# The opening of a fused attention and token-mixing kernel: eight score pairs in one written order for all engines

## The chip, the cores and the metric

The kernel runs on one core of one Trainium2 chip. A core has TensorE (PE; its weight loads are listed as PEld), VectorE (DVE), ScalarE (ACT), GpSimd (POOL) and SyncE (SP, which here only issues DMAs). The metric is the device time of one execution in microseconds (us), lower is better, as the median of several runs. Times inside a run count from the start of its span, which goes from the first to the last instruction.

## What is computed

Two blocks follow each other, for 8 batches of 3200 tokens, 256 columns wide:

```python
# u, v: (8, 3200, 256), z: (8, 3200, 64), float32
scores = (1 / 3200) * z @ z.transpose(0, 2, 1)
attn = np.maximum(scores, 0.0) ** 2
x = u * (attn @ v)                       # gated attention
wq, wk = x @ w_q, x @ w_k                # w_q, w_k: (256, 64)
W_tok = 0.125 * einsum('bsd,btd->bst', wq, wk)
mixed = einsum('bst,btd->bsd', W_tok, x)
out = np.maximum(mixed, 0.0) @ w_out     # w_out: (256, 256)
```

## The kernel before

**Tiles.** The 3200 tokens of a batch are 25 tiles of 128 rows. Columns of the score matrix are taken in groups of 512 (six, and one of 128). For one group, a score tile is 128 x 512: z of one row tile against z of the group's columns, over 64 entries. Two score tiles make a pair, which fills one PSUM buffer of 128 x 1024 float32; there are three such buffers (tag `ps`). Scores use z transposed, kept twice in `zT` (in partitions 0 to 63 and 64 to 127), so that the two tiles of a pair use the two halves of TensorE's rows.

**One pair** n passes four steps, which this text names by a letter and the pair's number:

- s (`scores`, L275): 64-row matmuls into a `ps` buffer.
- e (`first_stage`): relu and scaling into `g`, float32, on ScalarE (L287) or VectorE (L289). It frees the `ps` buffer.
- q (`second_stage`): the square, float16 into `at`, on ScalarE (L298) or GpSimd (L300). Where the score tile's transpose serves a later group, a DMA on SP's queue (L317) transposes it right behind.
- m (`second_product`, L333): `at` times v, accumulated over all tiles of the group in two PSUM banks, `acc0` and `acc1`. A tile makes four products of 128 x 256.

After a group's last product the gate (L463 to L466) multiplies by u, and the token-mixing work of the second block is worked in later.

**Order.** The schedule is written by hand: every engine takes its instructions in the order in which the program emits them, and semaphores are added for the data and the buffers. A loop over phases k emits, in each, some score pairs, their e, the q of the pairs of the phase before, and products of earlier pairs. From phase 3 on, products run as 64-row matmuls in two lanes, with score pairs between them. Loads and casts of later data are put on a list by phase (`due`). Products of the first group come in portions of 2, 4, 4, 5, 5 and 5 tiles (`first_sizes`), from phase 1 on.

**The opening.** z of the first batch comes in four chunks of 4, 6, 7 and 8 tiles (`ZCH`), which cover tiles 0 to 3, 12 to 17, 18 to 24 and 4 to 11; the first group takes its tiles in this order. Per chunk c there are three steps: z (`cast_first`, L113: two casts to float16, one for each copy), t (`turn_first`, L122: one TensorE transpose per tile) and c (the copy into `zT`, L126). Chunks 0 and 1 are turned in `acc0` and `acc1`, chunks 2 and 3 in `ps` buffers. So s0 and s1 need c0, s2 to s4 need c1, s5 to s7 need c2. v of the first batch is loaded in four DMAs with a cast, issued by GpSimd (L101).

The program emits: the identity, the four z loads (on SP), v tiles 0 to 3, then z0, t0, c0, z1, z2, v 12 to 17, z3, v 18 to 24, v 4 to 11. Phase 0 emits s0 s1, e0 e1, t1 c1, q0 q1. Phase 1: s2 s3 s4, e2 e3 e4, t2 c2, q2 q3 q4, m0. Phase 2: s5 s6 s7, e5 e6 e7, t3 c3, m1 m2. Phase 3 begins with the first u load on SP's queue, s8 (pair 8), e8, q5 q7 (GpSimd) and q6 (ScalarE), then products of pairs 3 and 4 with s9 and s10 between them. ScalarE has e0 c1 q0 e2 q2 q4 e5; VectorE has c0 e1 e3 e4 c2 e6 e7 c3; GpSimd has q1 and q3, and all casts of z2 and z3. The casts of z0 are on VectorE and ScalarE, those of z1 on ScalarE and GpSimd.

`zeros` is a 128 x 256 tile used later as a filler operand; GpSimd clears it in phase 11 (L206).

Of the kernel before, what the change touches and what calls it, by code (L numbers as in the profile page):

```python
# [9 lines left out]
FP16 = mybir.dt.float16  # L10
# [6 lines left out]
def kernel(  # L17
# [10 lines left out]
    nc = tc.nc  # L28

    B, S, D = u.shape  # L30
    dqk = z.shape[2]
    dh = moe_w_q.shape[1]
    P = 128
    NT = S // P
    ND = D // P
    W = 512
# [5 lines left out]
    LAG = 2  # L42
# [20 lines left out]
    pat = ctx.enter_context(tc.tile_pool(name="pat", bufs=NAT))  # L63
# [4 lines left out]
    pps = ctx.enter_context(tc.tile_pool(name="pps", bufs=3, space=bass.MemoryType.PSUM))  # L68
# [5 lines left out]
    def acc_tile(half, name, dtype=FP32):  # L74
        n = W if dtype == FP32 else 2 * W
        return pacc.tile([P, n], dtype, tag=f"acc{half}", name=name)

    ctx.enter_context(tc.manual_schedule())

    zT, vs, us, xs, xTs, qks, ks, hacc, hss, rts, zds = ({} for _ in range(11))  # L80
# [5 lines left out]
    ZCH = [(0, 4), (12, 6), (18, 7), (4, 8)]  # L86
# [8 lines left out]
    def load_first_z():  # L95
        for n0, nn in ZCH:
            z32[n0] = px.tile([P, nn, dqk], FP32, tag="x_sb", name="z32")
            nc.sync.dma_start(out=z32[n0][:], in_=rows(z, 0)[:, n0 : n0 + nn, :])

    def load_first_v(n0, nn):  # L100
        nc.gpsimd.dma_start(out=vs[0][:, n0 : n0 + nn, :], in_=rows(v, 0)[:, n0 : n0 + nn, :])  # L101

    def cast_first(c):
        n0, nn = ZCH[c]
        casts = [
            (nc.vector.tensor_copy, nc.scalar.copy),
            (nc.scalar.copy, nc.gpsimd.tensor_copy),
            (nc.gpsimd.tensor_copy, nc.gpsimd.tensor_copy),
            (nc.gpsimd.tensor_copy, nc.gpsimd.tensor_copy),
        ][c]  # L110
        zd0[c] = pat.tile([P, nn, 2, dqk], FP16, tag="at", name="zd")
        for half, cast in enumerate(casts):
            cast(out=zd0[c][:, :, half, :], in_=z32[n0][:])  # L113

    def turn_first(c):
        n0, nn = ZCH[c]
        if c < 2:
            tp = acc_tile(c, "ztp", FP16)
        else:
            tp = pps.tile([P, 4 * W], FP16, tag="ps", name="ztp")  # L120
        for i in range(nn):
            nc.tensor.transpose(  # L122
                tp[:, ts(i, P)], zd0[c][:, i, :, :].rearrange("p a k -> p (a k)"), ident
            )
        copy = nc.scalar.copy if c == 1 else nc.vector.tensor_copy
        copy(out=zT[0][:, ds(n0 * P, nn * P)], in_=tp[:, 0 : nn * P])  # L126

# [48 lines left out]
    def load_u(b, gi):  # L178
        n0, nn = starts[gi] // P, widths[gi] // P
        us[b, gi] = pu.tile([P, 4, D], FP32, tag="u_sb", name="u_sb")  # L180
        nc.sync.dma_start(out=us[b, gi][:, 0:nn, :], in_=rows(u, b)[:, n0 : n0 + nn, :])
# [22 lines left out]
    def clear(*tiles_):  # L204
        for tile_ in tiles_:
            nc.gpsimd.memset(tile_, 0.0)  # L206
# [57 lines left out]
    def scores(p0):  # L264
        pair = tiles[p0 : p0 + 2]
        sc = ps_tile("sc")
        ats = [[], []]
        for h, (b, gi, tis) in enumerate(pair):
            w = widths[gi]
            half = h * dqk  # L270
            for i in range(W // w):
                ti = tis[min(i, len(tis) - 1)]
                ats[h].append((i * w, h, w, b, ti, starts[gi], half))
        for at, h, w, b, ti, gs, half in sorted(ats[0] + ats[1]):
            nc.tensor.matmul(  # L275
                out=sc[:, h, at : at + w],
                lhsT=zT[b][half : half + dqk, ds(z_at(b, h) + ti * P, P)],
                rhs=zT[b][half : half + dqk, ds(z_at(b, h) + gs, w)],
                start=True,
                stop=True,  # L280
            )
        return sc

    def first_stage(p0, sc, on_act):
        g = pg.tile([P, 2, W], FP32, tag="g", name="g")
        if on_act:
            nc.scalar.activation(out=g[:], in_=sc[:], func=RELU, scale=GSCALE)  # L287
        else:
            nc.vector.tensor_scalar(  # L289
                out=g[:], in0=sc[:], scalar1=0.0, scalar2=GSCALE, op0=AOP.max, op1=AOP.mult  # L290
            )
        return g

    def second_stage(p0, g, on_act):
        at = pat.tile([P, 2 * W], FP16, tag="at", name="at")
        out = at[:].rearrange("p (a w) -> p a w", a=2)
        if on_act:
            nc.scalar.square(out=out, in_=g[:])  # L298
        else:
            nc.gpsimd.tensor_mul(out=out, in0=g[:], in1=g[:])  # L300
        blocks = []
        for h, (b, gi, tis) in enumerate(tiles[p0 : p0 + 2]):
            for i, ti in enumerate(tis):
                made[b, gi, ti] = (at, h * W + i * widths[gi])
            gj = group_of(tis[0])
            if is_turned(gi, gj):
                blocks.append((b, gi, gj, tis[0] - starts[gj] // P, 1, h * W, (h + 1) * W))
        if len(blocks) == 2 and blocks[0][:3] == blocks[1][:3] and blocks[1][3] == blocks[0][3] + 1:
            blocks = [blocks[0][:4] + (2, blocks[0][5], blocks[1][6])]
        for b, gi, gj, n0, nn, c0, c1 in blocks:  # L310
            if (b, gi, gj) not in turned:
                bufs = {1: 3, 2: 4, 4: 1}[gj - gi]
                turned[b, gi, gj] = ptt.tile(
                    [P, 4, 4, P], FP16, tag=f"tt{gj - gi}", name=f"tt{gj - gi}", bufs=bufs
                )
            out = turned[b, gi, gj][:].rearrange("p n j t -> p (n j) t")
            nc.sync.dma_start_transpose(out=out[:, 4 * n0 : 4 * (n0 + nn), :], in_=at[:, c0:c1])  # L317
# [19 lines left out]
    def whole(banks):  # L337
        return [
            lambda i=i: i.emit(ALL, i.start, i.stop) for bank in banks for i in bank
        ]  # L340
# [80 lines left out]
    def second_product(b, gi, rows_, first, last):  # L421

        nj = widths[gi] // P
        split = is_split(b, gi)
        if first:
            for half in range(2 if split else (nj + 1) // 2):
                accs[half] = acc_tile(half, f"acc{half}")

        def item(ti, j, half):
            return Item(  # L430
                out=accs[half][:, ds((j % 2) * D, D)],
                lhsT=lambda r: weights(b, gi, ti, j, r),
                rhs=lambda r: vs[b][r, ti, :],
                start=(first and ti == rows_[0] and j % 2 == 0),
                stop=(last and ti == rows_[-1] and (j % 2 == 1 or j == nj - 1)),
            )

        if split:
            return [[item(ti, 0, half) for ti in rows_] for half in range(2)]
        return [  # L440
            [item(ti, j, half) for ti in rows_ for j in range(2 * half, min(2 * half + 2, nj))]
            for half in range(2)
        ]
# [268 lines left out]
    def due(k, fn):  # L712
        at_phase.setdefault(k, []).append(fn)
# [84 lines left out]
    now = [0]  # L798
    mixed_at = [-9]
    make_identity(nc, ident)  # L800
    load_first_z()
    load_first_v(0, 4)
    cast_first(0)
    turn_first(0)
    cast_first(1)
    cast_first(2)
    load_first_v(12, 6)
    cast_first(3)
    load_first_v(18, 7)
    load_first_v(4, 8)  # L810
    due(3, lambda: load_u(0, 0))
    due(6, load_weights)
    due(8, load_out_weights)
    due(10, cast_weights)
    due(11, lambda: clear(zeros[:], zr[:, NT, :], first_kx[0][:]))
    due(12, lambda: double_weights(0))
    due(14, lambda: double_weights(1))
    due(15, lambda: clear(*[t[:] for t in first_kx[1:]], *[t[0:dh, :] for t in hz]))
# [54 lines left out]
        key += "x" if mixing else "k" if keying else "p" if projecting else ""  # L873
        return shares_of[key][:n]

    made_by = []
    waiting = []
    produced = consumed = k = 0
    groups = [(b, gi) for b in range(B) for gi in range(NG)]
    left, steps, across = None, 0, False  # L880
    gate_pending = False
    while groups:
        now[0] = k
        for fn in at_phase.pop(k, []):
            fn()
        n = 4 if k == 0 else 6
        mixing = None
        if len(groups) <= 2 and NTILE - produced <= 4 and not key_due(k):
            while todo_mix:
# [34 lines left out]

        for p0, sc in fresh:
            stage(p0, sc)
        if k < 3:
            turn_first(k + 1)
        if k < 2:

            for i, (p0, g) in enumerate(staged):
                second_stage(p0, g, i != 1)
            staged = []
        if len(waiting) == 3:
            second_on_act = [False, True, k % 2 == 0]
        else:
# [10 lines left out]
        while asides:  # L947
            asides.pop(0)()

        if k == 0:  # L950
            k += 1
            continue
        ready = made_by[k - (1 if k < 3 else LAG)]
        b, gi = groups[0]
        if begins:
            group_begun(k, b, gi)
            need = ends[b, gi]
            scored = tiles[consumed:need]
            scored = [t for _, _, tis in scored for t in tis]
            left = [t for t in range(NT) if t not in scored]  # L960
            first_sizes = [2, 4, 4, 5, 5, 5] if k == 1 else []
        need = ends[b, gi]
        rest = len(left) + sum(len(tis) for _, _, tis in tiles[consumed:need])
        if first_sizes:
# [180 lines left out]
```

## Time and profile before

| | us |
|---|---|
| median of 3 runs (lowest to highest) | 796.01 (794.72 to 796.9) |
| profiled execution, time | 793.18 |
| profiled execution, span | 790.8 |
| TensorE busy in the span | 769.5 |
| first TensorE instruction (t0) | 3.39 |
| first TensorE instruction of phase 3 (s8) | 15.39 |
| first gate, TensorE's last product before it ends near | 26.3 |

In the profile a busy engine is one with an instruction in flight; matmuls are pipelined, so a group's duration holds the wait of its last result too. "idle before" is what the engine waited just ahead of a group, with what released it. The granted clock (PEclk) is that of TensorE, as a share of full speed. A row of a timeline joins neighbouring instructions of one kind: start, duration of the whole, engine, line, operation, written and read tiles, shapes, count. In a row of stretches each engine has its busy time and its count of instructions, in the order TensorE, weight loads, VectorE, ScalarE, GpSimd, then the granted clock, the DMA engines' share and GB/s.

### The profile page before, as it was taken

To read this page: it belongs to the slowest core of one execution; us is meant where nothing else is said; L and a number is where in the kernel's file an instruction comes from. 1 tells how busy PE (TensorE), PEld (TensorE's weight loads), DVE (VectorE), ACT (ScalarE), POOL (GpSimd) and SP (SyncE) were. 2 spreads that over 40 slices of the span, in tenths; PEclk is the share of its full clock that TensorE was granted. 3 is DMA by queue.
4 is the path that set the end of the run, shared out by engine and by line. 5 is a ranking of instruction groups with operands and counts; after the bars stand their busy time and mean duration, and the time that the engine had idled before them with its cause. 6 is when DMAs were issued, how large, how long until landed. Compare 5 with 4: busy or idle time off the path is not lost. (4 is left out here: it accounts for less than half of the span.)

```text
span 790.8 us, 28408 instructions
## 1 busy us (share of the span) xinstructions
PE 769.5 (97%) x12590; PEld 658.3 (83%) x12590; DVE 470.4 (59%) x455; ACT 559.8 (71%) x656; POOL 552.6 (70%) x364
## 2 busy tenths in 40 slices
PE   7999999999999999999999999999999999999996
PEld 4777878887888888889878997899988998887884
DVE  5655566646655567555756457655575646665444
ACT  6766677776778776685867657758687877675465
POOL 7888698667766587774869658885677536876350
PEclk9999999999999999999999999999999999999999
DMA  8999799984999869995799949899489994988526
GB/s 170 179 210 206 124 201 194 190 185 82 237 184 216 173 157 216 231 229 138 171 214 235 241 114 177 222 188 262 113 216 187 228 229 97 189 193 165 157 61 257
DMA packets 276266, 147.03 MB, mean 186 GB/s; under 512 B 252080, under 2 KB 255664, under 8 KB 276144
## 3 DMA queue, kind: packets, MB, share of 16 engines
q1 hardware_dynamic: 275424, 143.33, 84.8%
q0 software_dynamic: 576, 1.64, 1.3%
q8 instruction: 98, 1.61, 0.9%
q10 hardware_dynamic: 144, 0.26, 0.1%
q14 instruction: 24, 0.20, 0.1%
HBM read 59.38 MB, written 26.21 MB: 108 GB/s over the span
## 5 line engine op out<-in xcount | busy, mean ns | idle before, releaser
L289 DVE TENSOR_SCALAR g<-sc 128x1024 f32<-128x1024 f32 x338 | 411.3, 1222 | 265.0 <-PE sc L275 235.8
L333 PE MATMUL acc<-v_sb,at 64*128 64x256 f16 (+1 forms) x7387 | 482.8, 269 | 3.6 <-POOL at L300 1.4
L300 POOL TENSOR_TENSOR at<-g 128x1024 f16<-128x1024 f32 x239 | 446.7, 1893 | 12.8 <-DVE g L289 12.0
L333 PEld LDWEIGHTS <-at 64*128 64x128 f16 (+1 forms) x7387 | 388.7, 94 | 68.4 <-PE acc L333 18.4
L298 ACT ACTIVATE at<-g 128x1024 f16<-128x1024 f32 x229 | 236.7, 1054 | 17.2 <-DVE g L289 16.2
L466 POOL TENSOR_TENSOR x_sb<-gt,u_sb 128x512 f16<-128x512 f32 x48 | 61.2, 1275 | 195.0 <-ACT gt L463 180.8
L333 PE MATMUL acc<-v_sb,tt 64*128 64x256 f16 (+1 forms) x2540 | 179.0, 269 | 0.0
L275 PE MATMUL sc<-zT 64*128 64x512 f16 (+1 forms) x1104 | 168.2, 346 | 3.2 <-ACT g L287 1.6
L287 ACT ACTIVATE g<-sc 128x1024 f32<-128x1024 f32 x130 | 133.0, 1023 | 41.0 <-PE sc L275 35.4
L333 PEld LDWEIGHTS <-tt 64*128 64x128 f16 (+1 forms) x2540 | 135.4, 94 | 10.1
L275 PEld LDWEIGHTS <-zT 64*128 64x128 f16 x1104 | 60.0, 94 | 11.1 <-issue 3.5
L600 ACT ACTIVATE rt<-mx 128x1024 f16<-128x1024 f32 x47 | 47.8, 1023 | 27.3 <-PE mx L579 25.3
L463 ACT COPY gt<-acc 128x512 f32<-128x512 f32 x48 | 28.1, 586 | 46.8 <-PE acc L333 46.7
L333 PE MATMUL fo<-wo,rt 64*128 64x256 f16 (+1 forms) x688 | 59.4, 269 | 1.3 <-DVE g L289 0.7
L661 ACT ACTIVATE fo<-fo 128x1024 f32<-128x1024 f32 (+2 forms) x44 | 43.6, 999 | 20.0 <-PE fo L333 19.6
L501 ACT CAST qk<-qk 128x512 f16<-128x512 f32 x47 | 27.5, 585 | 40.7 <-PE qk L333 40.4
L333 PE MATMUL qk<-x_sb,kx 64*128 64x256 f16 x368 | 55.0, 269 | 0.8 <-DVE g L289 0.8
L333 PEld LDWEIGHTS <-rt 64*128 64x128 f16 (+1 forms) x688 | 41.1, 94 | 13.4 <-issue 3.2
L464 DVE TENSOR_TENSOR x_sb<-acc,u_sb 128x512 f16<-128x512 f32 x48 | 33.1, 690 | 27.4 <-PE acc L333 24.5
L333 PEld LDWEIGHTS <-kx 64*128 64x128 f16 (+1 forms) x386 | 36.2, 94 | 7.1 <-DMA kx<-ql 0.7
L333 PE MATMUL qk<-xT_sb,wkq 64*128 64x512 f16 (+1 forms) x90 | 31.7, 376 | 0.8 <-DMA xT_sb<-x_sb 0.8
L333 PE MATMUL qk<-xT_sb,wqk 64*128 64x512 f16 (+1 forms) x94 | 30.1, 376 | 0.0
(79 smaller groups left out, 260.3 us busy)
## 6 DMA issues: line engine op xcount, KB each, us to landing
u_sb<-in_u_dram SPq DMA_DIRECT2D x48, 512.0 KB, 5.1
out_dram<-fo SPq DMA_DIRECT2D x45, 512.0 KB, 3.6
piece<-in_v_dram SPq DMA_DIRECT2D x42, 512.0 KB, 4.6
piece<-in_z_dram SPq DMA_DIRECT2D x7, 512.0 KB, 5.6
tt<-at SPq DMA_TRANSPOSE x162, 4.9
piece<-in_z_dram SPq DMA_DIRECT2D x7, 288.0 KB, 5.7
out_dram<-fo SPq DMA_DIRECT2D x5, 256.0 KB, 2.7
u_sb<-in_u_dram SPq DMA_DIRECT2D x8, 128.0 KB, 3.3
```

What stands on the lines that cost most here:

```text
L275: nc.tensor.matmul(out=sc[:, h, at : at + w], lhsT=zT[b][half : half + dqk, ds(z_at(b, h) + ti * P, P)], rhs=zT[b][half : half + dqk, ds(z ...
L287: nc.scalar.activation(out=g[:], in_=sc[:], func=RELU, scale=GSCALE)
L289: nc.vector.tensor_scalar(out=g[:], in0=sc[:], scalar1=0.0, scalar2=GSCALE, op0=AOP.max, op1=AOP.mult)
L298: nc.scalar.square(out=out, in_=g[:])
L300: nc.gpsimd.tensor_mul(out=out, in0=g[:], in1=g[:])
L333: return nc.tensor.matmul(out=self.out, lhsT=self.lhsT(rows), rhs=self.rhs(rows), start=start, stop=stop)
L463: nc.scalar.copy(out=upper[:], in_=accs[1][:])
L464: nc.vector.tensor_mul(out=x[:, 0:n], in0=accs[0][:, 0:n], in1=ug[:, 0:n])
L466: nc.gpsimd.tensor_mul(out=x[:, n : 2 * n], in0=upper[:], in1=ug[:, n : 2 * n])
L501: nc.scalar.copy(out=qks[b, gi][:, 0:gw], in_=out)
L600: nc.scalar.activation(out=out, in_=ps[:], func=RELU)
L661: nc.scalar.mul(out=flat_out[:, sl], in_=part, mul=FINAL_SCALE)
```

## The change

The opening, up to s7, is no longer emitted by phases 0 to 2 but by a new function `opening`, which reads one string of words. A word is a step (z, t, c, v, s, e, q, m), a number, and the engine (A ScalarE, D VectorE, P GpSimd); for z the digit between them is the copy, and "w10" is ten products of zeros on TensorE into `acc1` (128 x 256 each). `turn_first` is parted into the transposes and `place_first`, the copy. The loop then starts at phase 3 with the counters that phases 0 to 2 left.

What differs in order: ten products of zeros ahead of t0 and three behind it; t1 and c1 ahead of s0; t2 and m0 ahead of s4, t3 and m1 ahead of s5, m2 ahead of s7 (per engine; the words of different engines only stand side by side). The v loads of tiles 12 to 17 and 18 to 24 stand ahead of z2's casts on GpSimd, the last v load behind z3's casts. c1 goes from ScalarE to VectorE, q1 from GpSimd to ScalarE, e3 from VectorE to ScalarE. `zeros` is cleared on VectorE at the start instead of on GpSimd in phase 11.

```diff
--- before.py
+++ after.py
@@ -75,6 +75,11 @@
         n = W if dtype == FP32 else 2 * W
         return pacc.tile([P, n], dtype, tag=f"acc{half}", name=name)
 
+    OPENING = """
+        v0 z00D z01A w10 t0 w2 w1 c0D z10A z11P t1 c1D v1 s0 s1 e0A v2 e1D z20P z21P q0A s2
+        e2D q1A z30P z31P s3 e3A t2 m0 s4 c2D q2A v3 e4D q3P t3 m1 c3D s5 e5A q4A s6 e6D m2
+        s7 e7D
+    """
     ctx.enter_context(tc.manual_schedule())
 
     zT, vs, us, xs, xTs, qks, ks, hacc, hss, rts, zds = ({} for _ in range(11))
@@ -100,30 +105,29 @@
     def load_first_v(n0, nn):
         nc.gpsimd.dma_start(out=vs[0][:, n0 : n0 + nn, :], in_=rows(v, 0)[:, n0 : n0 + nn, :])
 
-    def cast_first(c):
+    cast_by = {"A": nc.scalar.copy, "D": nc.vector.tensor_copy, "P": nc.gpsimd.tensor_copy}
+    ztp = {}
+
+    def cast_first(c, half, by):
         n0, nn = ZCH[c]
-        casts = [
-            (nc.vector.tensor_copy, nc.scalar.copy),
-            (nc.scalar.copy, nc.gpsimd.tensor_copy),
-            (nc.gpsimd.tensor_copy, nc.gpsimd.tensor_copy),
-            (nc.gpsimd.tensor_copy, nc.gpsimd.tensor_copy),
-        ][c]
-        zd0[c] = pat.tile([P, nn, 2, dqk], FP16, tag="at", name="zd")
-        for half, cast in enumerate(casts):
-            cast(out=zd0[c][:, :, half, :], in_=z32[n0][:])
+        if half == 0:
+            zd0[c] = pat.tile([P, nn, 2, dqk], FP16, tag="at", name="zd")
+        cast_by[by](out=zd0[c][:, :, half, :], in_=z32[n0][:])
 
     def turn_first(c):
         n0, nn = ZCH[c]
         if c < 2:
-            tp = acc_tile(c, "ztp", FP16)
-        else:
-            tp = pps.tile([P, 4 * W], FP16, tag="ps", name="ztp")
+            ztp[c] = acc_tile(c, "ztp", FP16)
+        else:
+            ztp[c] = pps.tile([P, 4 * W], FP16, tag="ps", name="ztp")
         for i in range(nn):
             nc.tensor.transpose(
-                tp[:, ts(i, P)], zd0[c][:, i, :, :].rearrange("p a k -> p (a k)"), ident
-            )
-        copy = nc.scalar.copy if c == 1 else nc.vector.tensor_copy
-        copy(out=zT[0][:, ds(n0 * P, nn * P)], in_=tp[:, 0 : nn * P])
+                ztp[c][:, ts(i, P)], zd0[c][:, i, :, :].rearrange("p a k -> p (a k)"), ident
+            )
+
+    def place_first(c, by):
+        n0, nn = ZCH[c]
+        cast_by[by](out=zT[0][:, ds(n0 * P, nn * P)], in_=ztp[c][:, 0 : nn * P])
 
 
 
@@ -798,21 +802,11 @@
     now = [0]
     mixed_at = [-9]
     make_identity(nc, ident)
-    load_first_z()
-    load_first_v(0, 4)
-    cast_first(0)
-    turn_first(0)
-    cast_first(1)
-    cast_first(2)
-    load_first_v(12, 6)
-    cast_first(3)
-    load_first_v(18, 7)
-    load_first_v(4, 8)
     due(3, lambda: load_u(0, 0))
     due(6, load_weights)
     due(8, load_out_weights)
     due(10, cast_weights)
-    due(11, lambda: clear(zeros[:], zr[:, NT, :], first_kx[0][:]))
+    due(11, lambda: clear(zr[:, NT, :], first_kx[0][:]))
     due(12, lambda: double_weights(0))
     due(14, lambda: double_weights(1))
     due(15, lambda: clear(*[t[:] for t in first_kx[1:]], *[t[0:dh, :] for t in hz]))
@@ -873,17 +867,62 @@
         key += "x" if mixing else "k" if keying else "p" if projecting else ""
         return shares_of[key][:n]
 
-    made_by = []
-    waiting = []
-    produced = consumed = k = 0
+
+
     groups = [(b, gi) for b in range(B) for gi in range(NG)]
-    left, steps, across = None, 0, False
+    begun = {}
+
+    def warm(n):
+        if "x" not in begun:
+            begun["x"] = acc_tile(1, "sc")
+        for _ in range(n):
+            nc.tensor.matmul(
+                out=begun["x"][:, 0:D], lhsT=zeros[:, 0:P], rhs=zeros[:], start=True, stop=True
+            )
+
+    def opening(order):
+        sc, g = {}, {}
+        for word in order.split():
+            what, n, by = word[0], int(word[1:2]), word[2:]
+            if what == "z":
+                cast_first(n, int(by[0]), by[1])
+            elif what == "t":
+                turn_first(n)
+            elif what == "c":
+                place_first(n, by)
+            elif what == "v":
+                load_first_v(*[(0, 4), (12, 6), (18, 7), (4, 8)][n])
+            elif what == "s":
+                sc[n] = scores(2 * n)
+            elif what == "e":
+                g[n] = first_stage(2 * n, sc.pop(n), by == "A")
+            elif what == "q":
+                second_stage(2 * n, g.pop(n), by == "A")
+            elif what == "w":
+                warm(int(word[1:]))
+            elif what == "u":
+                load_u(0, 0)
+            elif what == "m":
+                ti = [t for x in tiles[2 * n : 2 * n + 2] for t in x[2]]
+                for fn in whole(second_product(0, 0, ti, n == 0, False)):
+                    fn()
+        return [(2 * n, g[n]) for n in sorted(g)]
+
+    load_first_z()
+    nc.vector.memset(zeros[:], 0.0)
+    waiting = opening(OPENING)
+    made_by = [4, 10, 16]
+    produced, consumed, k = 16, 6, 3
+    group_begun(1, 0, 0)
+    steps = 6
+    across = False
+    left, first_sizes = [], [4, 5, 5, 5]
     gate_pending = False
     while groups:
         now[0] = k
         for fn in at_phase.pop(k, []):
             fn()
-        n = 4 if k == 0 else 6
+        n = 6
         mixing = None
         if len(groups) <= 2 and NTILE - produced <= 4 and not key_due(k):
             while todo_mix:
@@ -924,13 +963,6 @@
 
         for p0, sc in fresh:
             stage(p0, sc)
-        if k < 3:
-            turn_first(k + 1)
-        if k < 2:
-
-            for i, (p0, g) in enumerate(staged):
-                second_stage(p0, g, i != 1)
-            staged = []
         if len(waiting) == 3:
             second_on_act = [False, True, k % 2 == 0]
         else:
@@ -947,10 +979,7 @@
         while asides:
             asides.pop(0)()
 
-        if k == 0:
-            k += 1
-            continue
-        ready = made_by[k - (1 if k < 3 else LAG)]
+        ready = made_by[k - LAG]
         b, gi = groups[0]
         if begins:
             group_begun(k, b, gi)
@@ -958,7 +987,6 @@
             scored = tiles[consumed:need]
             scored = [t for _, _, tis in scored for t in tis]
             left = [t for t in range(NT) if t not in scored]
-            first_sizes = [2, 4, 4, 5, 5, 5] if k == 1 else []
         need = ends[b, gi]
         rest = len(left) + sum(len(tis) for _, _, tis in tiles[consumed:need])
         if first_sizes:
```

## The prediction

> **What bounds the kernel now.** I read the page's busy table first, then stretches of the opening, then each engine's timeline up to 20 us. Times within the run count from the start of its span.
>
> ```profile
> PE 769.5 (97%) x12590; PEld 658.3 (83%) x12590; DVE 470.4 (59%) x455; ACT 559.8 (71%) x656; POOL 552.6 (70%) x364
> ```
>
> TensorE is the bound. Its idle 21 us (790.8 - 769.5) include 5.9 of the first 15.39 us (15.39 - 9.50 busy). The second row below is the stretch behind: 11.00 of 11.00 us busy.
>
> ```profile
> 0.00:15.39 15.39, 9.50 (x65) 5.36 (x66) 7.78 (x9) 9.03 (x10) 11.64 (x19) 1.00 0.79 153
> 15.39:26.39 11.00, 11.00 (x178) 8.26 (x179) 9.23 (x8) 9.36 (x10) 8.97 (x5) 1.00 1.08 168
> ```
>
> So a change of the opening is worth what it moves TensorE's first instruction of phase 3, score pair s8, now at 15.39, if the helpers then keep up. TensorE's timeline (start, duration, operation):
>
> ```profile
> 3.39 0.61 PE L122 MATMUL ztp<-ident,zd 128*128 128x128 f16 x4 [3.39 <-ACT zd L113]
> 4.51 1.04 PE L275 MATMUL sc<-zT 64*128 64x512 f16 x4 [0.52 <-DVE zT L126]
> 5.48 0.82 PE L122 MATMUL ztp<-ident,zd 128*128 128x128 f16 x6
> 7.19 1.46 PE L275 MATMUL sc<-zT 64*128 64x512 f16 x6 [0.89 <-ACT zT L126]
> 9.06 0.91 PE L122 MATMUL ztp<-ident,zd 128*128 128x128 f16 x7 [0.41 <-ACT g L287]
> 9.76 1.91 PE L333 MATMUL acc<-v_sb,at 128*128 128x256 f16 x8
> 11.60 0.82 PE L275 MATMUL sc<-zT 64*128 64x512 f16 x6
> 13.11 0.61 PE L122 MATMUL ztp<-ident,zd 128*128 128x128 f16 x8 [0.69 <-ACT g L287]
> 13.55 1.91 PE L333 MATMUL acc<-v_sb,at 128*128 128x256 f16 x16
> 15.39 0.61 PE L275 MATMUL sc<-zT 64*128 64x512 f16 x4
> ```
>
> Two things hold it. First, order: t1 stands behind s0 and s1, c1 follows it, so s2 to s4 come only at 7.19; t3 stands behind s7 and waits at 13.11 for the buffer that e5 leaves. Second, pace: 8 products at 9.76 take what 16 take at 13.55. Less a tail of 0.18 us these are 0.213 and 0.107 us each. The granted clock reads 1.00 in both stretches, so the durations have to be trusted, not that column. Half pace holds until 11.25, the last slow product.
>
> The helpers' rows give the other prices:
>
> ```profile
> 6.34 0.80 ACT L126 COPY zT<-ztp 128x768 f16<-128x768 f16 x1 [0.15 <-PE ztp L122]
> 16.81 1.99 ACT L298 ACTIVATE at<-g 128x1024 f16<-128x1024 f32 x2
> 10.54 0.61 DVE L126 COPY zT<-ztp 128x896 f16<-128x896 f16 x1
> 16.11 3.49 DVE L289 TENSOR_SCALAR g<-sc 128x1024 f32<-128x1024 f32 x3 [0.91 <-PE sc L275]
> 6.34 0.53 POOL L101 DMA_DIRECT2D v_sb<-in_v_dram  x1
> 9.04 3.76 POOL L300 TENSOR_TENSOR at<-g 128x1024 f16<-128x1024 f32 x2
> ```
>
> VectorE: a relu each 1.15 us, done after 1.22. ScalarE: an operation each 0.95, done after 1.02 (relu) or 1.06 (square). GpSimd: a square 1.88, a load's issue 0.53.
>
> **The change, part by part.** *Zeros.* The memset leaves GpSimd at 45.46 (0.32 us, under a busy TensorE: nothing gained) and goes to VectorE, which waits until 2.93 for z: hidden. No row has it on VectorE; between nothing and 0.32 us, I take 0.3 from 0.75, where the engines' first work starts. Without that cover it would delay z0 by as much.
>
> *Thirteen products of zeros*, at half pace 0.213 each. Ten run from 1.1 to 3.2, before t0 at 3.39: hidden. If the memset came 0.3 later they would end at 3.5, and t0 loses 0.1. Three run behind t0 (end 3.82) to 4.46; t1 could start at 4.25, so they cost 0.21. What they buy is the pace. It is now reached after at most 4.2 us (7.19 to 11.4) and at least 2.3 us (9.06 to 11.4) of nearly unbroken work; from 1.1 that makes 3.4 to 5.3. I take 4.5 and keep both ends, and 10.9, no gain, for a rival.
>
> [...]
>
> *The chain.* With 0.05 us from an end to the start that waits for it, and 0.13 when TensorE goes between 128-row and 64-row work (11.46 to 11.60): t1 4.46, done 5.0; c1, now on VectorE, 0.55 between the rows of 512 and 896 columns (ScalarE: 0.80), ends 5.58 instead of 7.14. s0 and s1 slip from 4.51 to 4.93 and 5.15: the price of t1 ahead. e0 (ScalarE) 5.38 to 6.40, e1 5.59 to 6.81. s2 runs at 5.63 (was 7.19); s3 waits for e0's buffer, 6.45. VectorE: e2 6.74 to 7.96, c2 to 8.50. ScalarE: q0 to 7.51, q1 to 8.47 (was GpSimd's, 1.88), e3 to 9.39, q2 to 10.36. TensorE: t2 6.86, m0 7.56, s4 at 8.56 for the buffer of e2; e4 9.01 to 10.23. t3 takes e3's buffer at 9.44 (was 13.11, by 3.7 the largest move), m1 9.88, c3 10.16 to 10.84; s5 10.89, s6 11.10; e5 11.33 to 12.35, e6 11.55 to 12.77; m2 11.45, s7 12.45, e7 12.90 to 14.12. **s8 starts at 12.67 instead of 15.39, 2.7 earlier.** ScalarE's load grows by 1.1 (q1 0.95, e3 0.95, c1 -0.80), VectorE's falls by 0.6, GpSimd's by 1.88.
>
> *What is late next.* q4 stands behind e5 and ends at 13.32 (was 11.72). In phase 3 pair 4's products need it after s9, 12.88, and eight products of pair 3 (0.43): a wait of some 0.06. s10 needs e7's buffer, 14.17. Phase 4 starts at 15.24 for 17.82: 2.6 kept. GpSimd: q5 follows e5, 12.40, q7 ends 16.16, only 0.8 before its present 16.94; phase 4 wants it at 16.53. Phases 5 and 6 come out at 18.03 and 20.83 (20.68 and 23.53 now). The same steps worked for the present kernel end 0.2 to 0.3 early (15.22, 17.59, 20.38), so some of the 2.6 is optimism of the method; I take **2.5 us**.
>
> *Queues passed.* On GpSimd two v loads (2 x 0.53) go ahead of z2's and z3's casts, which wait for landing anyway (z2 at 5.33); z3's casts start near 6.6 to 7.3 and t3 wants them at 9.44: hidden. The last v load stays near 8.5, lands by 17.7 (9.2 us), wanted at 18.9. On SP q4's transpose DMA, 1.6 later, delays the first u load behind it from 13.29 to 14.9; with 8.2 us, the longest landing of its kind early on, 23.1, wanted at 24.2 (26.69 less 2.5).
>
> ```profile
> v_sb<-in_v_dram POOLq DMA_DIRECT2D x1, 512.0 KB, 9.2
> z<-in_z_dram SPq DMA_DIRECT2D x1, 256.0 KB, 4.5
> ```
>
> **Sum.** The profiled execution has span 790.8 and time 793.18: less 2.5, 790.7. The median of the runs shown is 796.01, 2.8 above it; the same 2.5 less is **793.5**. A measurement of this kernel tells about 0.3% (2.4 us) from no change, and the forecast is right at that edge.
>
> **Rivals.** *The pace comes late.* If it rises at 6 or later, s0 to s3 run slow, s8 comes at 13.18, and the gain is 1.9; if the zeros bring nothing (10.9), s8 at 14.02, gain 1.2. Time some 794.4. For: between 5.5 and 8.5 work at half pace did not raise it. Against: that work had gaps, the zeros have none.
>
> *More than that.* In executions where the present kernel reaches full pace after 12, its phase 3 starts 0.5 later still by the same steps; with the rise at 4.0 in the new one the gain is 3.3: 792.7. For: only one execution is profiled, and the median is slower than it.
>
> *Given back.* GpSimd's squares lead phase 4 by only 0.37 us (16.16 against 16.53). If the squares start a little later TensorE waits there; the lead is then limited to the 0.3 to 0.8 by which q7 moved: 795.5. For: 11.64 us of GpSimd work in the opening, the most of the helpers. Against: 1.88 of it goes.
>
> *Slower: z3 shares the DMA engines with v.* The two v loads now start while z3 is still landing. The chain bears z3 until about 8.1 (two casts of 0.62, then t3 at 9.44); from there each us costs one, through t3, the last v load and q3, queued behind its casts on GpSimd. From 10.6 the gain is gone. If z3 waited for both v loads (832 KB kept, twice that read, 8.3 us at 200 GB/s from 5.3) it would land at 13.6: 3.0 later than that, 799.0. [...]
>
> **Chances.** Forecast 0.48 (its own range 2.0 to 3.2 us, 792.8 to 794.0), late pace 0.16, more 0.12, given back 0.12, slower 0.12. Over 0.3% faster: 0.42 of the forecast, all of "more", 0.02 of the late pace: 0.56. Slower by as much: 0.11 of the last, 0.02 of "given back": 0.13. Within: 0.31. The range goes from 791.6 (a gain of 4.4, both ends of the pace) to 796.6, and leaves out the slow end of z3.
>
> **What would show it.** Right: products of zeros from about 1.1, products of m0 0.107 us apart, s2 near 5.6, t3 near 9.4, s8 between 12.4 and 13.2, GpSimd's q7 before TensorE asks for pair 7, and later phases shifted by the same amount. Wrong: m0 at 0.213; a wait of t2 or t3 for casts on GpSimd, or of those for z; TensorE idle in phases 3 to 6; or an early lead gone by the first gate near 24.

## The result and the profile after

| | before | changed |
|---|---|---|
| median of 6 runs each | 796.38 us | 792.06 us |
| ratio of changed to before, 95% interval | | 0.9949, 0.9936 to 0.9962 |
| profiled execution, time | 793.18 | 792.58 |
| its span | 790.8 | 790.7 |
| s8 / s11 / s14 start | 15.39 / 17.82 / 20.68 | 12.26 / 14.91 / 17.78 |
| first record of full TensorE pace | 11.6 | 4.8 |

The changed kernel is faster, by 4.3 us (3.0 to 5.1 from the interval), yet the two profiled spans are alike. Both facts have to be explained. First TensorE's timeline of the changed kernel, which answers to the ten rows shown of before (between 9.09 and 14.91 six rows are left out):

```profile
1.07 2.31 PE L879 MATMUL sc<-zeros 128*128 128x256 f16 x10 [1.07 <-DVE zeros L912]
3.44 0.61 PE L124 MATMUL ztp<-ident,zd 128*128 128x128 f16 x4
3.84 0.85 PE L879 MATMUL sc<-zeros 128*128 128x256 f16 x3
4.74 0.52 PE L124 MATMUL ztp<-ident,zd 128*128 128x128 f16 x6
5.19 1.11 PE L279 MATMUL sc<-zT 64*128 64x512 f16 x6
6.70 0.39 PE L279 MATMUL sc<-zT 64*128 64x512 f16 x2 [0.40 <-ACT g L291]
7.12 0.55 PE L124 MATMUL ztp<-ident,zd 128*128 128x128 f16 x7
7.79 1.05 PE L337 MATMUL acc<-v_sb,at 128*128 128x256 f16 x8
8.77 0.39 PE L279 MATMUL sc<-zT 64*128 64x512 f16 x2
9.09 0.62 PE L124 MATMUL ztp<-ident,zd 128*128 128x128 f16 x8
12.04 0.82 PE L279 MATMUL sc<-zT 64*128 64x512 f16 x6
14.91 0.61 PE L279 MATMUL sc<-zT 64*128 64x512 f16 x4
```

The zeros begin at 1.07. m0, eight products, takes 1.05 us from 7.79 where it took 1.91: full pace. t3 runs at 9.09 instead of 13.11, right behind s4 (8.77). The row at 12.04 holds s7, s8 and s9; s11 starts at 14.91, 2.9 earlier than before. In the stretches up to s8 and behind it (busy time of TensorE, weight loads, VectorE, ScalarE, GpSimd) TensorE idles 1.84 us in the first, where it idled 5.9, and 0.09 in the second:

```profile
0.00:12.26 12.26, 10.42 (x78) 6.14 (x80) 7.23 (x10) 8.39 (x10) 7.74 (x17) 1.00 0.88 189
12.26:24.30 12.04, 11.95 (x184) 8.93 (x181) 11.18 (x11) 10.83 (x13) 10.94 (x6) 1.00 0.96 156
```

The helpers' rows: the memset on VectorE takes 0.17 us, c1 0.56; e3 runs on ScalarE from 8.59 to 9.60; the two v loads go ahead; z3's casts wait 0.27 for their landing; the next six squares on GpSimd run without a pause between them.

```profile
0.85 0.17 DVE L912 MEMSET zeros<- 128x128 uint32 x1 [0.85 <-PEq L1157]
5.30 0.56 DVE L130 COPY zT<-ztp 128x768 f16<-128x768 f16 x1 [0.79 <-PE ztp L124]
8.59 1.01 ACT L291 ACTIVATE g<-sc 128x1024 f32<-128x1024 f32 x1
4.51 1.06 POOL L106 DMA_DIRECT2D v_sb<-in_v_dram  x2
6.90 1.17 POOL L115 CAST zd<-z 128x512 f16<-128x512 f32 x2 [0.27 <-DMA z<-in_z_dram]
12.05 11.15 POOL L304 TENSOR_TENSOR at<-g 128x1024 f16<-128x1024 f32 x6 [0.48 <-ACT g L291]
```

Where did the lead go in this execution? It holds until 394 us. There TensorE waits 1.55 and 0.48 us (rows of TensorE, then of ScalarE). A first wait of 1.25 to 1.78 us stands at this place of the program in all five profiles of the two kernels:

```profile
392.93 1.25 PE L337 MATMUL acc<-v_sb,at 64*128 64x256 f16 x20
395.73 0.61 PE L279 MATMUL sc<-zT 64*128 64x512 f16 x4 [1.55 <-ACT g L291]
396.82 0.61 PE L337 MATMUL fo<-wo,rt 64*128 64x256 f16 x8 [0.48 <-DVE ha L539]
397.25 3.91 PE L337 MATMUL acc<-v_sb,at 64*128 64x256 f16 x36
...
393.71 1.04 ACT L141 CAST zr<-piece 128x1024 f16<-128x1024 f32 x1 [2.92 <-DMA piece<-in_z_dram]
394.67 1.01 ACT L291 ACTIVATE g<-sc 128x1024 f32<-128x1024 f32 x1
```

ScalarE waits 2.92 us for a piece of z; the relu that would free a `ps` buffer stands behind that cast. What follows costs more: the 36 products at 397.25 take 3.91 us, 0.11 us each, where the 20 at 392.93 take 0.06. The stretches (granted clock ahead of the last two columns) say why:

```profile
393.94:397.36 3.42, 1.39 (x19) 0.71 (x14) 1.00 (x3) 3.42 (x6) 0.69 (x2) 1.00 1.49 303
397.36:400.77 3.41, 3.41 (x35) 2.67 (x33) 1.14 (x2) 2.26 (x3) 3.41 (x4) 0.50 0.87 158
```

Behind a stretch in which TensorE was busy for 1.39 of 3.42 us, its granted clock was 0.50 for the next 3.41 us, which costs some 1.7 (half of it, an estimate from this row). A further 2 us go between 604 and 635 us, most of it behind a wait of 2.75 us of ScalarE for a piece of v ahead of a cast:

```profile
611.34 1.04 ACT L141 CAST v_sb<-piece 128x1024 f16<-128x1024 f32 x1 [2.75 <-DMA piece<-in_v_dram]
```

In the profiled execution of before there is neither a half clock in mid-run nor this second loss. One profile each was a poor pair to compare.

### The profile page after: what moved, and what is told of

It is laid out like the page before. It is cut to its first block, busy times and chain, and to the rows that moved or that the text cites. A ratio compares the mean times of both kernels' runs of the same rounds, so it can differ in the third digit from the quotient of the medians.

```text
span 790.7 us, 28435 instructions
## 1 busy us (share of the span) xinstructions
PE 772.2 (98%) x12603; PEld 659.5 (83%) x12603; DVE 471.2 (60%) x457; ACT 560.1 (71%) x656; POOL 550.5 (70%) x362
## 5 line engine op out<-in xcount | busy, mean ns | idle before, releaser
L279 PEld LDWEIGHTS <-zT 64*128 64x128 f16 x1104 | 59.6, 94 | 11.6 <-issue 5.7
L141 ACT CAST v_sb<-piece 128x1024 f16<-128x1024 f32 (+1 forms) x25 | 23.4, 936 | 10.4 <-DMA piece<-in_v_dram 10.4
```

What stands on the lines that cost most here:

```text
L279: nc.tensor.matmul(out=sc[:, h, at : at + w], lhsT=zT[b][half : half + dqk, ds(z_at(b, h) + ti * P, P)], rhs=zT[b][half : half + dqk, ds(z ...
```

## The experiments

Each expectation was written before the run. Ratios are to the kernel before, run beside it in the same set of runs. The changed kernel itself did not run in the set of old_engines, late_t3, late_t1 and fill_gap. "s11" is the start of the first score pair of phase 4 in the profile, "full pace" the first record of the full clock.

| run | s11 | full pace | median us, of it and of before beside it | ratio, 95% interval |
|---|---|---|---|---|
| b_again | 18.09 | 13.3 | 793.60, 794.65 | 0.9998 (0.9982 to 1.0015) |
| a_again | 14.84 | 4.8 | 789.83, 794.65 | 0.9944 (0.9922 to 0.9966) |
| no_zeros | 15.68 | 8.8 | 791.54, 794.65 | 0.9965 (0.9947 to 0.9983) |
| zeros_only | 17.68 | 6.0, half from 9.4 to 12.8 | 793.50, 794.65 | 0.9984 (0.9969 to 1.0) |
| old_engines | 16.30 | 6.9 | 793.01, 795.75 | 0.9968 (0.995 to 0.9985) |
| late_t3 | 16.59 | 6.2 | 792.52, 795.75 | 0.9962 (0.9946 to 0.9978) |
| late_t1 | 15.68 | 6.5 | 792.65, 795.75 | 0.9965 (0.995 to 0.9981) |
| fill_gap | 15.31 | 7.1 | 794.43, 795.75 | 0.9983 (0.9967 to 0.9999) |
| a_third | 15.29 | 6.0 | 790.44, 795.48 | 0.9938 (0.9922 to 0.9954) |
| z_pool | 15.29 | 6.9 | 788.30, 795.48 | 0.9911 (0.9895 to 0.9926) |
| v_late | 15.29 | 6.1 | 789.89, 795.48 | 0.9924 (0.9902 to 0.9946) |
| b_z_pool | 17.62 | 11.1 | 793.77, 795.99 | 0.9976 (0.9964 to 0.9988) |

**b_again and a_again: the two kernels once more, unchanged.**

> The kernel before, unchanged, for its spans and clocks in several executions. The profiled spans of before and after are alike (790.8 and 790.7) though the medians differ by 4.3 us. Theory A (the clock and late DMA waits in mid-run differ from execution to execution, and the one profiled execution of before was a good one): spans of the timed executions spread from 791 to 795, most at 793 or more, with a mean granted clock of 0.997 or less in the long ones. Theory B (time outside the span differs): spans all near 790.8, and time less span 4 us or more. Either way s8 starts near 15.4.

> The changed kernel, unchanged, for a second profile. Theory A: s8 near 12.0 again and the lead at the first gate 2.9 us; the half-clock stretch near 397 us and the wait of TensorE near 612 us may be absent. If both come back at the same places, the change itself brings them (theory C: part of the lead is given back at fixed places). Time 0.9949 of before, within 0.003.

Spans of the 40 executions of before in this set go from 789.9 to 795.2, with a median of 792.2; the profiled 790.8 lies low among them. Theory A holds in the main, though its "most at 793 or more" was too high, and some long executions (794.1, 792.2) have a mean clock of 0.998. Time less span is 2.3 us for before and 1.9 to 2.0 for the changed kernel, so theory B holds a small part, 0.3 to 0.4 us. In a_again the same wait near 394 us came; TensorE was idle for 1.34 us of the first stretch shown (3.41 less 2.07), and the granted clock was 1.00 in the next.

```profile
393.95:397.36 3.41, 2.07 (x29) 1.50 (x30) 1.93 (x3) 3.41 (x6) 1.40 (x2) 1.00 1.15 227
397.36:400.78 3.42, 3.42 (x66) 3.39 (x63) 1.44 (x2) 2.36 (x3) 3.42 (x3) 1.00 1.09 249
```

Its span was 787.8. The wait of ScalarE near 612 us moved to 616, 1.6 us for TensorE: theory C holds for that one, which all three profiles of the changed kernel have (1.1 us in a_third), and the two of before don't.

**no_zeros and zeros_only: which half brings it.**

```diff
-        v0 z00D z01A w10 t0 w2 w1 c0D z10A z11P t1 c1D
+        v0 z00D z01A t0 c0D z10A z11P t1 c1D
```

```diff
     cast_first(0)
+    warm(10)
     turn_first(0)
+    warm(3)
```

> The changed kernel without its thirteen products of zeros. Theory order (the written order brings most of it): full pace comes at 7.5 to 11 and s8 starts at 12.4 to 13.3, 0.4 to 1.3 later than the 12.04 of the changed kernel; time 792.5 to 793.4. Theory pace (the zeros bring most): s8 at 14 or later, time 794.5 or more.

> The kernel before with the products of zeros (ten ahead of t0, three behind it, the memset on VectorE at the start) and no other change. Theory order: full pace comes near 5, but c1, the buffers and the late t3 hold s8 at 14.2 to 14.7, 0.7 to 1.2 earlier than 15.39; time 795.2 to 795.7. Theory pace: s8 at 13 or earlier, time 793.5 or less.

Without the zeros s11 starts at 15.68, still 2.1 earlier than 17.82. With the zeros alone it is 17.68, 0.1 earlier. The order brings most; that part of the expectation held. These are single profiles, and the place of the clock's rise differs between them. But the zeros alone brought even less than expected, and the rows show why (TensorE, then stretches, of zeros_only):

```profile
5.50 0.71 PE L122 MATMUL ztp<-ident,zd 128*128 128x128 f16 x6
7.11 0.82 PE L275 MATMUL sc<-zT 64*128 64x512 f16 x6 [0.89 <-ACT zT L126]
8.97 0.56 PE L122 MATMUL ztp<-ident,zd 128*128 128x128 f16 x7 [1.04 <-ACT g L287]
9.36 1.88 PE L333 MATMUL acc<-v_sb,at 128*128 128x256 f16 x8
...
5.96:9.37 3.41, 1.48 (x18) 0.79 (x16) 2.49 (x3) 3.33 (x5) 1.76 (x4) 1.00 0.54 84
9.37:12.79 3.42, 3.26 (x17) 1.40 (x15) 1.81 (x3) 2.66 (x3) 3.41 (x5) 0.50 0.83 127
```

Full pace came at 5.96; with the old order's two waits (0.89 and 1.04 us) TensorE was busy for 1.48 of the next 3.41 us, and behind that the granted clock was 0.50 for 3.42 us, just for m0: 1.88 us. In this profile the early pace, which the order didn't keep, was worth nearly nothing. On top of the order the zeros are worth 0.4 to 0.8 us (15.68 less 15.29 or 14.84).

**old_engines, late_t3, late_t1: the parts of the order.**

```diff
-  t1 c1D v1 s0 s1 ... s2 e2D q1A ... s3 e3A t2 ... v3 e4D q3P
+  t1 c1A v1 s0 s1 ... s2 e2D ... s3 e3D t2 ... v3 q1P e4D q3P
```

```diff
-  q3P t3 m1 c3D s5 e5A q4A s6 e6D m2 s7 e7D
+  q3P s5 e5A q4A s6 e6D s7 e7D t3 c3D m1 m2
```

```diff
-  c0D z10A z11P t1 c1D v1 s0 s1 e0A v2
+  c0D z10A z11P s0 s1 e0A t1 c1D v1 v2
```

> The changed kernel with the old engines for three steps: c1 on ScalarE, q1 on GpSimd (behind the third v load, ahead of q3), e3 on VectorE; the order of the rest and the zeros stay. Theory order-of-TensorE (the early t1 and t3 bring the lead): s11, which starts at 14.9 in the changed kernel and 17.8 before, comes 0.3 to 0.6 later, at 15.2 to 15.5. Theory engines (moving load off VectorE and GpSimd brings it): s11 at 16.4 or later. Time +0.3 to +0.6 against +1.5.

> The changed kernel with t3, c3 and m1 put back behind s7, as before; engines and zeros as changed. Theory order-of-TensorE: this is the largest move; s11 comes 0.7 to 1.2 later, at 15.6 to 16.1, with a wait of t3 for the buffer that e5 leaves. Theory engines: s11 at 15.2 or earlier.

> The changed kernel with t1 and c1 put back behind s0 and s1, and the v loads as changed; the zeros stay ahead of s0. Theory chain: s0 and s1 come 0.5 earlier and s2 0.3 to 0.7 later, e0 and e1 earlier; both meet at the buffers, and s11 stays within 0.3 of 14.9. Rival (c1 early is what counts): s11 0.6 or more later.

The expectations counted from 14.9, a profile with full pace at 4.8; these three have it at 6.2 to 6.9. Set against 15.29 (a_third and z_pool, full pace at 6.0 and 6.9): t3 back costs 1.3 us, the engines back 1.0, t1 back 0.4. The order of the sizes is as expected, and all three are larger; late_t1 lies between its theory and the rival, and old_engines, with 16.30, just short of its rival's 16.4. In late_t3 t3 waits 0.63 us for e5's relu, as expected; two score pairs ahead of it wait too (for e3's and e4's):

```profile
10.02 0.39 PE L279 MATMUL sc<-zT 64*128 64x512 f16 x2 [0.27 <-ACT g L291]
10.86 0.39 PE L279 MATMUL sc<-zT 64*128 64x512 f16 x2 [0.45 <-DVE g L293]
11.88 0.61 PE L124 MATMUL ztp<-ident,zd 128*128 128x128 f16 x8 [0.63 <-ACT g L291]
```

In old_engines VectorE has three relus in a row from 6.49, and t3 waits for it; then m1 waits for q1 on GpSimd. The engines count as part of the order, more than the 0.3 to 0.6 expected:

```profile
10.03 0.61 PE L124 MATMUL ztp<-ident,zd 128*128 128x128 f16 x8 [0.27 <-DVE g L293]
10.93 1.05 PE L337 MATMUL acc<-v_sb,at 128*128 128x256 f16 x8 [0.29 <-POOL at L304]
...
6.49 3.49 DVE L293 TENSOR_SCALAR g<-sc 128x1024 f32<-128x1024 f32 x3 [2.04 <-PE sc L279]
```

In the ratios the three can't be told from each other; the shares above rest on one profile each.

**v_late: the v loads behind the casts of z, as before.**

```diff
-  c1D v1 s0 s1 e0A v2 e1D z20P z21P q0A ... z30P z31P s3
+  c1D s0 s1 e0A e1D z20P z21P v1 q0A ... z30P z31P v2 s3
```

> The changed kernel with the second v load behind z2's casts and the third behind z3's on GpSimd, as before. Theory hidden: the casts of z3 wait for their landing anyway, s11 within 0.2 of the changed kernel at the same start of full pace, time within 0.8 us. Rival (v shares the DMA engines with z): z3's casts start earlier than 6.9, s11 0.3 or more earlier. Rival on the other side (v comes late): TensorE waits for v in phases 2 to 4, s11 or s14 later by 0.5 or more.

s11 at 15.29, as in a_third; z3's casts start at 7.34 (7.18 there). The place of the v loads changes nothing that can be seen, and the rival of z3 coming late behind v has no support in any profile here.

**fill_gap: products of zeros in the wait near 394 us.**

```diff
+                items[-1:-1] = [z_] * pad
...
-                emits += lanes(part, across, True, {})
+                emits += lanes(part, across, True, {}, 14 if k == 89 and part is banks else 0)
```

> The changed kernel with fourteen products of zeros per lane, added to the accumulators just ahead of their last products in phase 89, where TensorE waits 1.5 us near 394 us for ScalarE. [...]

The filling did not pay. The profile has it (28 products, 1.69 us) and no half clock behind it (the mean of the execution is 1.0), but 0.46 and 0.74 us of waiting are left:

```profile
393.58 1.69 PE L337 MATMUL acc<-zeros,at 64*128 64x256 f16 x28
396.06 0.39 PE L279 MATMUL sc<-zT 64*128 64x512 f16 x2 [0.46 <-DVE ha L545]
397.19 0.61 PE L337 MATMUL fo<-wo,rt 64*128 64x256 f16 x8 [0.74 <-DVE g L293]
```

The median was 794.43 (the profiled execution, 791.55, was the fastest), some 3 us above the changed kernel by ratio, and half of the 12 executions still had a mean clock of 0.997 or less. The profile shows one more loss, a wait of 1.96 us at 695 for a DMA of keys (0.2 to 0.5 in the other profiles). Whether the filling brings that is open.

**a_third, z_pool and b_z_pool: taking the wait away.** All mid-kernel casts of z go to GpSimd, which is idle at that place:

```diff
-            copy = nc.gpsimd.tensor_copy if now[0] % 2 == 0 else nc.scalar.copy
+            on_pool = src is z or now[0] % 2 == 0
+            copy = nc.gpsimd.tensor_copy if on_pool else nc.scalar.copy
```

> The changed kernel, unchanged, beside the next two on the same chip. [...] Time 0.9949 of before, within 0.002.

> The changed kernel with all mid-kernel casts of z on GpSimd (four of fourteen pieces of 16 tiles and three of 9 tiles leave ScalarE). Theory wait: TensorE's gap of 1.25 to 1.9 us near 394 us comes from ScalarE waiting there for a z piece ahead of a relu; on GpSimd, idle there until 396, the wait holds nobody. The gap and the half-clock stretch behind it go; median 1.2 to 3 us below the changed kernel of the same call. Rival (the DMA is what is late, and the next reader of the piece waits as long): the gap stays, or others of the same size come, median within 0.8 us.

> The kernel before with all mid-kernel casts of z on GpSimd, and its old opening. Open is where the rest of the 4.3 to 5.0 us comes from: TensorE's lead behind the opening is 2.5 to 3.0 us, the time outside the span is 0.4 us shorter. Theory gap (the old kernel's executions lose more at the gap near 394 us and the half clock behind it): with the gap gone the old kernel gains 3 to 4 us, ratio 0.995 to 0.9962, and comes within 3.4 us of the changed kernel with the same edit (0.9911). Theory elsewhere: it gains 2.1 us as the changed kernel did, ratio 0.9970 to 0.9980, and 4.5 us or more stay between the two.

The wait is gone from TensorE (z_pool: the score pair follows the products at once, while the cast runs on GpSimd):

```profile
392.73 1.25 PE L338 MATMUL acc<-v_sb,at 64*128 64x256 f16 x20
393.82 0.38 PE L280 MATMUL sc<-zT 64*128 64x512 f16 x2
...
393.83 1.04 POOL L142 CAST zr<-piece 128x1024 f16<-128x1024 f32 x1
```

z_pool beats both kernels: 788.30 against 790.44 for the changed kernel beside it, 2.1 us less, and its slowest execution (788.99) is faster than that kernel's fastest (789.33). None of its 5 executions, nor of the 12 of b_z_pool, had a mean clock of 0.997 or less; of before 53 of 103 had, of the changed kernel 6 of 18. The count is rough: the mean also holds a half clock behind TensorE's last product, where TensorE has nothing left to do: 0.50 for the last 0.99 us in the profile of before, for the last 0.83 in that of the changed kernel. At 0.996 or less it is 40 of 103 and none of 18. The old kernel gained 1.9 us (0.0024 of 796) by the same edit, so the casts of z cost both about the same, which speaks against the wait as the source of what the change gained beyond the opening: 5.2 us stay between the two (0.9976 less 0.9911, from two sets of runs). One sight of what else varies is in b_z_pool, where the gate waits 3.02 us for u at 82 us (VectorE; 1.37 in a_third, for its own products), and TensorE 1.47 behind it:

```profile
82.23 0.69 DVE L465 TENSOR_TENSOR x_sb<-acc,u_sb 128x512 f16<-128x512 f32 x1 [3.02 <-DMA u_sb<-in_u_dram]
82.97 1.27 PE L334 MATMUL acc<-v_sb,at 64*128 64x256 f16 x20 [1.47 <-DVE x_sb L465]
```

## Why the prediction was right, and its size too small

*Direction, place and range held.* 792.06 lies inside 791.6 to 796.6, and the gain is clear of 0.3%.

*The opening was the right place and nearly the right size.* s11 was put at 15.24 and s14 at 18.03; six profiles with this opening (v_late among them) have s11 at 14.84 to 15.31, the first 17.78 for s14. The lead over before (17.82) is 2.5 to 3.0 us where the steps said 2.6 and the forecast took 2.5. s2, put at 5.63, came at 5.8 to 6.2.

*One step had the wrong cause.* t3 was put at 9.44, for the buffer that e3 leaves at 9.39. It came at 9.09 in the first profile, while e3 was still running (8.59 to 9.60), and at 9.47 in a_third (e3 there 8.96 to 9.96): right behind s4, without a wait for e3. In the first profile s4 was 0.2 us later than said (8.77 for 8.56) and t3 0.35 earlier, so that part of the agreement in s11 is two errors that cancel.

*The zeros.* Start at 1.07 (said: 1.1) and memset 0.17 us (said: 0.3, hidden) held. Ten took until 3.3 to 3.4, not 3.2, and t0 slipped by at most 0.05: nothing.

*The pace.* Full pace at 4.8 in two profiles, 6.0 to 7.1 in four; the forecast took 4.5 with 3.4 to 5.3 as bounds from the rows. So the late-pace rival happened, in part, in most profiles, for 0.4 us of the lead where its steps gave 0.5 (s8 at 13.18 for 12.67). Nothing in the rows says why the same opening reaches full pace at different times.

*Queues passed.* v_late shows the v loads free of cost (s11 at 15.29, as in a_third). q4's transpose did move the first u load, to 15.43 (said: 14.9), with no wait of the first gate for it in the profiles.

*GpSimd.* The squares kept ahead: behind s8 TensorE lost 0.09 us in 12. That rival fell.

*More than that* was to come from a late full pace of the old opening. b_again had it at 13.3 and s11 0.27 us later than in the first profile (said: 0.5), b_z_pool at 11.1 and s11 0.20 earlier. So the place of the rise moves the lead both ways, from 2.3 to 3.3 us over all these profiles, and adds little on the mean.

*What was mis-sized* is the term of the sum that was left at nothing: "the same 2.5 less" from the median, as if a lead behind the opening simply moved the end. The medians differ by 4.3, 4.8 and 5.0 us in three sets of runs. Measured apart: 2.5 to 3.0 in the opening, 0.3 to 0.4 outside the span (though b_z_pool, with the old opening, has 2.0 there too, so the opening may not be its cause). The rest, 1 to 2 us, shows in no profile. In a_again, where the clock stayed up, the lead over the profiled execution of before is 2.98 us at the first gate (23.71 for 26.69) and 3.06 at the last, and the span is 3.0 shorter; in a_third it is 2.53 and 3.36. The last gate on VectorE in before, then in a_again:

```profile
765.97 0.69 DVE L464 TENSOR_TENSOR x_sb<-acc,u_sb 128x512 f16<-128x512 f32 x1 [2.99 <-PE acc L333]
762.91 0.69 DVE L468 TENSOR_TENSOR x_sb<-acc,u_sb 128x512 f16<-128x512 f32 x1 [2.99 <-PE acc L337]
```

So the rest lies in executions of before that are slower than its profiled ones: 790.8 and 791.1 against a median of 792.2. The half clock takes part in it, 1.7 us a time: by the rough counts above its share is larger for before by 0.18 (0.997 or less) or 0.39 (0.996 or less), which makes 0.3 to 0.7 us on the mean, by estimate. b_z_pool speaks against the wait near 394 us as the main part. What remains was not found: single profiles show waits for u, v and z at 81, 394 and 612 us that come and go by 1 to 2 us between executions, a slow execution of before was never profiled, and no run here says why before should meet more of them.

That 792.06 lies inside the range is in part luck: the lower end, 791.6, stood for an early pace of the new opening beside a late one of the old, and the new one's pace came late in most profiles.

## What to carry to other kernels

Where one engine is busy throughout, a written order for the first microseconds is priced by when that engine's steady stream begins; move first what frees the buffers its next steps wait for, and give each helper only what the chain allows. Raising the clock early was worth 0.1 us here where the order left TensorE idle for 1.93 of the next 3.41 us (zeros_only), and 0.4 to 0.8 with the new order. A cast that waits for a DMA should stand on the engine that nobody is waiting for at that moment (2.1 us in z_pool), and two profiles of kernels that differ by half a percent say nothing on the end of the run until several executions' spans and clocks are beside them.

## What had not been expected of the hardware

In two of the profiles shown here a stretch with long waits of TensorE was followed by one at half clock. In the changed kernel the granted clock was 0.50 from 397.36 to 400.77, behind 3.42 us with 2.03 idle; in zeros_only from 9.37 to 12.79, behind 3.41 us with 1.93 idle. Elsewhere it stayed up: in a_again it was 1.00 behind 1.34 us of idle time in 3.41, in the profile of before 1.00 with 1.71 idle between 397.32 and 400.74, and in fill_gap the mean of the execution was 1.0 with a wait of 1.96 us ending at 696.64. So a similar wait at the same place of the program cost nothing more in a_again and some 1.7 us more in the changed kernel's first profile; these profiles don't say what decides it.

Products of zeros, all of them zero times zero, went with an early rise: between 1.41 and 4.82 us of the changed kernel TensorE is busy for 3.30 us, some 2.8 of them with zeros, and the first record of full pace is at 4.8 (6.0 in a_third). Without them, in no_zeros, it is at 8.8.
